# An S4D convolution and a feed-forward layer on one core: the kernel products take turns over the column tiles, in fewer steps

## The chip, the cores and the metric

The kernel runs on one NeuronCore of a Trainium2 chip. The metric is the device time of one execution in microseconds. The core has a matrix engine (PE, TensorE), which multiplies into PSUM, a vector engine (DVE), a scalar engine (ACT), GpSimd (POOL) and a queue engine (SP). In this kernel SP and POOL start nearly all transfers. Each engine takes its instructions in the order of the built program and waits on semaphores for the others.

## The reference

The input is 2048 tokens of 576 channels, all float32. Two residual stages follow each other, each modulated by rows of `silu(c) @ w_mod`:

```python
h = _layernorm(x) * (1 + ca) + sa
x = x + ga * _A_ref(h, ...)        # S4D: a convolution along the tokens, per channel
h = _layernorm(x) * (1 + cb) + sb
x = x + gb * _B_ref(h, w1, w2)     # relu(h @ w1) @ w2, with 4608 hidden units
```

The convolution kernel of a channel is `K[l] = 2 Re sum_n C[n] exp(A[n] dt l)` over 128 states n and 2048 positions l.

## The kernel before

**The convolution kernel K.** A position is split as l = 32 a + b. For one channel, K is a matrix product over the 128 states: `W2` (128 states x 32 values of b) times `W1` (128 states x values of a), once for the real parts and once for the imaginary parts (r = 0 and 1), added up in PSUM. The 576 channels are cut into 12 half groups h of 48 channels. A half group's 48 channels stand as 4 x 12: dd = 0 to 3 picks one of four column tiles of the matrix array (32 columns, 32 PSUM partitions each) and q = 0 to 11 is the place along the row. So a half group is 96 matmuls of 128 x 32 weights. The moving side has 16 columns for each block of 512 positions: 16, 32 or 48.

**Where these products run.** Block 0 of K (16 columns) is made first, by `products` of `KGen` (lines 252 to 269), before the feed-forward layer starts. Blocks 1 to 3 are made by `rest` (lines 383 to 475) beside the feed-forward layer: in feed-forward block 0 the half groups 0 to 5 with 48 columns (blocks 1, 2, 3) in turn with the half groups 6 to 11 with 16 columns (block 1); in feed-forward block 1 the half groups 6 to 11 with 32 columns (blocks 2, 3). Before its products a half group's `W1r` is rotated on DVE (`rot`, lines 403 to 415: two products of 1536 elements, an addition and a subtraction of 768). Its `W2r`, `W` and `Zr` are loaded by POOL's queue. ScalarE copies the products out of PSUM into `ker` (line 450), and when six half groups are done POOL's queue stores them.

**The convolution.** `conv` (line 855) transforms, multiplies spectra (`product`, line 970), and transforms back, for token blocks of 512; block s + 1 is convolved beside feed-forward block s.

**The feed-forward layer.** `ffn` (line 1246) goes through 4 token blocks of 36 hidden tiles. One tile is 14 matmuls into `hps` (line 1305) and 14 into five accumulators `acc` (line 1330), each 128 x 512, with operands split into a high and a low part (`xh`, `xl`, `hh`, `hl`). ScalarE writes `hh` (line 1310), DVE `hl` (line 1311); the second buffer of `hps` comes free with `hl`.

**What sets the order.** The side work is a generator per block. `step` (line 1340) is called every seven feed-forward matmuls and takes pieces from the generator until the work done reaches a rate (2.3 units per step in block 0, 1.85 in block 1). A piece that yields a number counts that many units (its DVE time). A piece that yields `None` is a piece of matrix work: it counts 0.7, and a step takes at most two of them. Behind that a scheduler of the language orders the instructions of each engine. The PSUM tag `cps` has one buffer in this stage, so a new tile of `kps` waits for the ScalarE copy of the one before.

Of the kernel before, what the change touches and what calls it, by code (L numbers as in the profile page):

```python
# [10 lines left out]
F32 = mybir.dt.float32  # L11
F32R = mybir.dt.float32r
I32 = mybir.dt.int32
AF = mybir.ActivationFunctionType
# [4 lines left out]
P = 128  # L19
# [21 lines left out]
def strips(t, k):  # L41

    w = t.shape[1] // k
    return bass.AP(tensor=t.tensor, offset=t.offset, ap=[[w, P], [P * w, k], [1, w]])


class KGen:
# [204 lines left out]
    def products(self, ps, W1, W2, u, between):  # L252

        for q in range(12):
            if q % 6 == 3:
                for _ in range(2):
                    next(between, None)
            for dd in range(4):
                ch = dd * 12 + q
                for r in range(2):  # L260
                    self.mm = self.kept(
                        self.nc.tensor.matmul(  # L262
                            ps[32 * dd : 32 * dd + 32, 12 * u + q, :],
                            W2[:, r, :, ch],
                            W1[:, u, :, r, ch],
                            start=(r == 0),
                            stop=(r == 1),
                        )
                    )
# [113 lines left out]
    def rest(self, psum, items, beside=iter(())):  # L383


        nc, k = self.nc, self.k
        v = nc.vector.tensor_tensor
        kes, rows = {}, {}
        most = 16 * max(len(blocks) for _, blocks in items)
        with ExitStack() as ctx:  # L390
            pt = k.pool(ctx, f"kr{items[0][1][0]}")

            def load(h):
                W2 = pt.tile([P, 2, 32, H], F32, tag="W2", bufs=2, name=f"W2r_{h}")
                W0 = pt.tile([P, 16, 2, H], F32, tag="W0", bufs=2 if most == 48 else 1, name=f"W0_{h}")
                Z = pt.tile([P, 2, 2, H], F32, tag="Z", bufs=2, name=f"Zr_{h}")
                d = nc.gpsimd.dma_start
                d(out=W0.rearrange("p (y a) r c -> p y (a r c)", y=2), in_=strips(k.W1d[h], 2))
                d(out=Z.rearrange("p i r c -> p (i r c)"), in_=k.Zd[h])
                k.gate = d(out=W2.rearrange("p r (y b) c -> p (r y) (b c)", y=2), in_=strips(k.W2d[h], 4))  # L400
                return W2, W0, Z

            def rot(out, X, Z, i):
                cb = [P, 32, H]
                flat = "p a r c -> p (a r) c"
                T = pt.tile([P, 16, 2, H], F32, tag="T", name="T")
                zr, zi = (Z[:, i, r].unsqueeze(1).broadcast_to(cb) for r in range(2))
                v(T.rearrange(flat), X.rearrange(flat), zi, op=ALU.mult)
                yield 1.75
                v(out.rearrange(flat), X.rearrange(flat), zr, op=ALU.mult)  # L410
                yield 1.75
                v(out[:, :, 0], out[:, :, 0], T[:, :, 1], op=ALU.subtract)  # L412
                yield 0.95
                v(out[:, :, 1], out[:, :, 1], T[:, :, 0], op=ALU.add)
                yield 0.95

            def rots(W1, W0, Z, blocks):
                a = [W1[:, 16 * i : 16 * i + 16] for i in range(len(blocks))]
                if blocks[0] == 1:
                    yield from rot(a[0], W0, Z, 0)  # L420
                    if len(blocks) > 1:
                        yield from rot(a[1], W0, Z, 1)
                        yield from rot(a[2], a[0], Z, 1)
                else:
                    yield from rot(a[0], W0, Z, 1)
                    yield from rot(a[1], a[0], Z, 0)

            def products(h, W1, W2, blocks):
                na = 16 * len(blocks)
                key = (h // 6, blocks)  # L430
                if key not in kes:
                    kes[key] = pt.tile([P, na, 72], F32, name=f"ker_{h}")
                ke = kes[key]
                for half in range(2):
                    ps = psum.tile([P, 6, na], F32, tag="cps", bufs=1, name="kps")
                    for q in range(6):
                        for dd in range(4):
                            ch = dd * 12 + 6 * half + q
                            for r in range(2):
                                nc.tensor.matmul(  # L440
                                    ps[32 * dd : 32 * dd + 32, q, :],
                                    W2[:, r, :, ch],
                                    W1[:, :na, r, ch],
                                    start=(r == 0),
                                    stop=(r == 1),
                                )
                        if q == 2:
                            yield None
                    q0 = 12 * (h % 6) + 6 * half
                    nc.scalar.activation(  # L450
                        ke[:, :, q0 : q0 + 6], ps.rearrange("p q a -> p a q"), AF.Copy
                    )
                    yield None
                rows[key] = rows.get(key, 0) + 1
                if rows[key] == 6:
                    yield -1
                    for i, s in enumerate(blocks):
                        self.store(
                            s, h // 6, ke[:, 16 * i : 16 * i + 16].rearrange("p a q -> p (a q)"),
                            nc.gpsimd,  # L460
                        )

            nxt = load(items[0][0])
            yield -1
            prev = iter(())
            for i, (h, blocks) in enumerate(items):
                W2, W0, Z = nxt
                W1 = pt.tile([P, most, 2, H], F32, tag="W1", bufs=2, name=f"W1r_{h}")
                yield from spread(rots(W1, W0, Z, blocks), prev, len(blocks))
                if i + 1 < len(items):  # L470
                    nxt = load(items[i + 1][0])
                prev = products(h, W1, W2, blocks)
                if i + 2 == len(items):
                    yield next(beside, -1)
            yield from both(prev, beside)


def spread(a, b, n):

    for i, w in enumerate(a):  # L480
        yield w
        if i % n == n - 1:
            yield next(b, 0.0)
    yield from b


class Body:
# [20 lines left out]
    def v(self, *args, **kw):  # L508
        return self.kept(self.nc.vector.tensor_tensor(*args, **kw))  # L509
# [982 lines left out]
def both(a, b):  # L1492

    while True:
        n = 0
        for g in (a, b):
            for w in g:
                n = 1
                yield w
                break  # L1500
        if not n:
            return
# [58 lines left out]
```

## Time and profile before

| | us |
|---|---|
| runs: lowest, median, highest (3 runs) | 1362.56, 1365.63, 1367.47 |
| profiled execution: from the first to the last instruction (span) | 1360.4 |
| what the median run has beyond that span | 5.2 |
| matmuls busy (PE), weight loads busy (PEld) | 1226.0, 973.7 |
| vector engine, scalar engine, GpSimd busy | 871.4, 503.5, 195.3 |
| products of line 440: matmul records, busy | 3456, 77.4 |
| products of line 262: matmul records, busy | 2304, 40.3 |

The profiled execution's own time is known as its span, from its first to its last instruction. The runs were timed by themselves and hold what lies around it.

A matmul of two float32 operands stands in the trace as two matmul records, each with a weight load of its own; one of the feed-forward layer (`fp32r`) as one. So the 1728 matmuls of line 440 are 3456 records. A row of the timeline joins equal instructions that follow each other: its start, its length to the end of the last one, and how many. In brackets stands how long the engine idled before it and who ended the wait; "issue" means that the engine waited for nothing that the profile shows. The ends of matmuls are modelled, so the starts are the surer times. Rows of the stage view give a stretch, its length, then the busy time and the instructions of each engine, the granted clock, the share of the transfer engines and GB/s.

### The profile page before, as it was taken

Reading aid. Unit: us, or ns where it says so; the run is one execution under the profiler, and the core shown is the slowest. Engines: PE = TensorE matmul, PEld = TensorE weight load, DVE = VectorE, ACT = ScalarE, POOL = GpSimd, SP = SyncE. Lnnn points to the kernel's source line nnn. Section 1 sums busy time; section 2 is a strip of 40 time slices with the busy share of each in tenths; the row PEclk is TensorE's granted clock in tenths of the full one; section 3 lists DMA queues with packets and bytes.
Section 4 is the critical chain, followed back from the end, with each engine's and each line's share of the span. In section 5 each row is a group of like instructions: output and inputs, shape, how many; then the busy total and the mean of one; then the engine's idle time right before and its main releaser. Section 6 shows DMA issues by size and latency. Waiting matters only on the chain.

```text
span 1360.4 us, 26053 instructions
## 1 busy us (share of the span) xinstructions
PE 1226.0 (90%) x10608; PEld 973.7 (72%) x10608; DVE 871.4 (64%) x1351; ACT 503.5 (37%) x1014; POOL 195.3 (14%) x271
## 2 busy tenths in 40 slices
PE   5125797999999987999999999999999999999998
PEld 3124565777787766777777887787888888888886
DVE  5978997998878698469737986266999222111111
ACT  7986234222224311622233225333322253233321
POOL 1777231111120100021101100100010000000000
PEclk9557899999999998999999999999999999999999
DMA  6666499988898755699689894677997567666651
GB/s 196 243 246 241 135 356 366 331 292 275 292 344 289 265 199 207 205 362 316 236 278 342 294 362 143 206 245 233 317 348 259 178 177 211 198 195 197 197 174 61
DMA packets 132424, 340.47 MB, mean 250 GB/s; under 512 B 22352, under 2 KB 22672, under 8 KB 132304
## 3 DMA queue, kind: packets, MB, share of 16 engines
q1 hardware_dynamic: 105200, 215.21, 48.9%
q0 software_dynamic: 26816, 123.01, 24.6%
q8 instruction: 83, 1.36, 0.4%
q10 hardware_dynamic: 288, 0.59, 0.1%
q14 instruction: 37, 0.30, 0.1%
HBM read 258.55 MB, written 80.22 MB: 249 GB/s over the span
## 4 chain that ended last, share of the span: by engine, by line
PE 70%; DVE 11%; DMA 10%; issue 4%; ACT 2%; POOL 1%; SPq 0%; DVEq 0%; ACTq 0%; POOLq 0%
PE acc L1330 28%; PE hps L1305 28%; PE kps L440 5%; PE ps_f L757 4%; PE kps L262 3%; DVE T L509 2%; DVE Y L509 2%; DMA Ua<-Ud 2%; DMA Ud<-U 2%; DVE k L133 1%; PE ps_i L998 1%; DMA h<-in_x_dram 1%; DMA Ka<-Rd 1%; DMA Zr<-Zd 1%; DMA W1d<-W 1%
## 5 line engine op out<-in xcount | busy, mean ns | idle before, releaser
L1330 PE MATMUL acc<-hh,w 128*128 128x512 f32 x1296 | 422.1, 400 | 0.3 <-DVE w L509 0.3
L1305 PE MATMUL hps<-xh,w 128*128 128x512 f32 x1152 | 394.3, 402 | 4.4 <-ACT xh L1061 3.5
L1311 DVE SCALAR_TENSOR_TENSOR hl<-hps,hh 128x512 fp32r<-128x512 f32 x144 | 99.0, 688 | 291.3 <-ACT hh L1310 291.0
L1330 PEld LDWEIGHTS acc<-hh,w 128*128 128x128 f32 x1296 | 242.1, 188 | 52.5 <-DVE w L509 0.9
L1330 PE MATMUL acc<-hl,w 128*128 128x512 f32 x720 | 278.7, 399 | 0.0
L1305 PEld LDWEIGHTS hps<-xh,w 128*128 128x128 f32 x1152 | 217.4, 190 | 52.1 <-ACT xh L1061 4.7
L1305 PE MATMUL hps<-xl,w 128*128 128x512 f32 x576 | 230.8, 401 | 0.2 <-DVE xl L1066 0.2
L1310 ACT ACTIVATE hh<-hps 128x512 fp32r<-128x512 f32 x144 | 86.0, 598 | 354.6 <-PE hps L1305 347.0
L1283 ACT ACTIVATE w<-r 128x576 fp32r<-128x576 f32 x144 | 98.6, 686 | 217.9 <-issue 168.4
L1330 PEld LDWEIGHTS acc<-hl,w 128*128 128x128 f32 x720 | 135.3, 188 | 28.2
L1305 PEld LDWEIGHTS hps<-xl,w 128*128 128x128 f32 x576 | 109.2, 190 | 24.8 <-DVE xl L1066 1.5
L1305 PE MATMUL hps<-xs,w 128*128 128x512 f32 x288 | 97.2, 417 | 14.3 <-DVE hl L1311 14.0
L1276 ACT ACTIVATE w<-r 128x640 fp32r<-128x640 f32 x142 | 104.0, 733 | 12.4 <-DMA r<-in_w_dram 12.4
L262 PE MATMUL kps<-W,W 128*32 128x16 f32 x2304 | 40.3, 215 | 71.5 <-POOL W L59 47.3
L262 PEld LDWEIGHTS kps<-W,W 128*32 128x32 f32 x2304 | 37.9, 150 | 76.2 <-POOL W L59 49.7
L440 PEld LDWEIGHTS kps<-W1r,W2r 128*32 128x32 f32 x3456 | 68.4, 146 | 30.7 <-issue 16.8
L509 DVE TENSOR_TENSOR Y<-Y,T 128x1152 f32<-128x1152 f32 x64 | 84.7, 1351 | 0.2
L440 PE MATMUL kps<-W1r,W2r 128*32 128x48 f32 (+2 forms) x3456 | 77.4, 238 | 7.0 <-DVE W1r L412 3.3
L1305 PEld LDWEIGHTS hps<-xs,w 128*128 128x128 f32 x288 | 52.8, 190 | 28.3 <-DVE hl L1311 17.1
L758 ACT ACTIVATE Z<-ps_f 128x288 f32<-128x288 f32 x104 | 42.4, 407 | 63.1 <-PE ps_f L757 62.3
L509 DVE TENSOR_TENSOR w<-r,w 128x512 fp32r<-128x512 f32 (+2 forms) x108 | 57.9, 572 | 8.6 <-ACT w L1283 8.6
L509 DVE TENSOR_TENSOR W<-Z 128x576 f32<-128x576 f32 x52 | 37.1, 752 | 29.3 <-ACT Z L758 29.3
(216 smaller groups left out, 1362.8 us busy)
## 6 DMA issues: line engine op xcount, KB each, us to landing
r<-in_w_dram SPq DMA_DIRECT2D x144, 320.0 KB, 4.2
r<-in_w_dram SPq DMA_DIRECT2D x144, 288.0 KB, 3.7
w<-L1d SPq DMA_DIRECT2D x108, 320.0 KB, 3.0
w<-L2d SPq DMA_DIRECT2D x108, 288.0 KB, 3.2
W2r<-W2d POOLq DMA_DIRECT2D x18, 1536.0 KB, 9.4
W2d<-W SPq DMA_DIRECT2D x10, 1536.0 KB, 7.4
W<-W1d POOLq DMA_DIRECT2D x18, 768.0 KB, 8.9
Ua<-Ud POOLq DMA_DIRECT2D x12, 1152.0 KB, 10.3
```

Of the source, the lines that this page charges most:

```text
L133: self.nc.vector.scalar_tensor_tensor(f[:, i].rearrange(pair, u=2), th, float(slot), k[:, i].rearrange(pair, u=2), op0=ALU.mult, op1=ALU.s ...
L262: self.nc.tensor.matmul(ps[32 * dd : 32 * dd + 32, 12 * u + q, :], W2[:, r, :, ch], W1[:, u, :, r, ch], start=(r == 0), stop=(r == 1),)
L440: nc.tensor.matmul(ps[32 * dd : 32 * dd + 32, q, :], W2[:, r, :, ch], W1[:, :na, r, ch], start=(r == 0), stop=(r == 1),)
L509: return self.kept(self.nc.vector.tensor_tensor(*args, **kw))
L757: kept(nc.tensor.matmul(o, fc[:, n2, c, :], src(n2), start=True, stop=True))
L758: nc.scalar.activation(Z[:, n2, c], ps[:, :PC], AF.Copy)
L1276: nc.scalar.activation(w[:, 0], r, AF.Copy)
L1283: nc.scalar.activation(w[:, 0:D], r2[g], AF.Copy)
L1305: nc.tensor.matmul(ps, a, x, start=(i == 0), stop=(i == 13))
L1310: nc.scalar.activation(hh, ps, AF.Relu)
L1311: nc.vector.scalar_tensor_tensor(hl, ps, 0.0, hh, op0=ALU.max, op1=ALU.subtract)
L1330: nc.tensor.matmul(acc[i], a, x, start=(f == 0 and j in (0, 3, 6, 9, 12)), stop=(f == NF - 1 and j in (2, 5, 8, 11, 13)),)
```

## The change

In both places the loops over r and dd change places: each matmul now goes to another column tile than the one before, and the r = 1 matmul of a channel comes four matmuls after its r = 0. In `rest`, a half group with 16 or 32 columns now has one PSUM tile of 12 x 16 or 12 x 32 and one step (96 matmuls, one copy); one with 48 columns has two tiles of 6 x 48 and two steps (48 matmuls each). Before, every half group had two tiles, two copies and four steps of 24 matmuls.

```diff
@@ products @@
-            for dd in range(4):
-                ch = dd * 12 + q
-                for r in range(2):
+            for r in range(2):
+                for dd in range(4):
+                    ch = dd * 12 + q
                     self.mm = self.kept(
@@ rest @@
-                for half in range(2):
-                    ps = psum.tile([P, 6, na], F32, tag="cps", bufs=1, name="kps")
-                    for q in range(6):
-                        for dd in range(4):
-                            ch = dd * 12 + 6 * half + q
-                            for r in range(2):
+                n = 12 if na < 48 else 6
+                for q1 in range(0, 12, n):
+                    ps = psum.tile([P, n, na], F32, tag="cps", bufs=1, name="kps")
+                    for q in range(n):
+                        for r in range(2):
+                            for dd in range(4):
+                                ch = dd * 12 + q1 + q
                                 nc.tensor.matmul(
                                     ps[32 * dd : 32 * dd + 32, q, :],
                                     W2[:, r, :, ch],
...
-                        if q == 2:
-                            yield None
-                    q0 = 12 * (h % 6) + 6 * half
+                    q0 = 12 * (h % 6) + q1
                     nc.scalar.activation(
-                        ke[:, :, q0 : q0 + 6], ps.rearrange("p q a -> p a q"), AF.Copy
+                        ke[:, :, q0 : q0 + n], ps.rearrange("p q a -> p a q"), AF.Copy
                     )
                     yield None
```

The lines behind it move up by one (1305 becomes 1304, 1330 becomes 1329, 1311 becomes 1310), the matmul of `rest` is at line 441 after the change.

How this moves the instructions is seen in the built order. First TensorE at the first half group with 16 columns, beside the second hidden tiles of feed-forward block 0 (the last column is partitions x columns and the number of matmuls). Before:

```order
L440 MATMUL kps<-W1r_2947,W2r_2927 32x48 x48
L1305 MATMUL hps<-xh_2777,w_2987 128x512
L1305 MATMUL hps<-xl_2778,w_2987 128x512
L1305 MATMUL hps<-xh_2777,w_2987 128x512
L440 MATMUL kps<-W1r_3032,W2r_3026 32x16
L1330 MATMUL acc_0_3035<-hl,w_2997 128x512
...
L1330 MATMUL acc_0_3035<-hh,w_3138 128x512 x2
L440 MATMUL kps<-W1r_3032,W2r_3026 32x16 x47
L1305 MATMUL hps<-xs_2779,w_3024 128x512 x2
L440 MATMUL kps<-W1r_3032,W2r_3026 32x16 x24
```

and after the change, at the same place:

```order
L441 MATMUL kps<-W1r_2947,W2r_2927 32x48 x48
L1304 MATMUL hps<-xh_2777,w_2987 128x512 x2
L1304 MATMUL hps<-xl_2778,w_2987 128x512
L441 MATMUL kps<-W1r_3032,W2r_3026 32x16 x4
L1304 MATMUL hps<-xh_2777,w_2987 128x512
L441 MATMUL kps<-W1r_3032,W2r_3026 32x16 x92
L1329 MATMUL acc_0_3035<-hl,w_2997 128x512
```

The half group's 96 matmuls stood in four pieces (1, 47, 24 and 24) between feed-forward matmuls, and now stand in two, of 4 and 92, close behind the 48-column half group. Over the whole program the runs of line 440 go from 65 to 39.

Second DVE, at the second spectral product (`Y_1`) of token block 1, between two writes of `hl`, for which the feed-forward matmuls wait. Before:

```order
L1311 SCALAR_TENSOR_TENSOR hl<-hps,hh 128x512
L509 TENSOR_TENSOR w_6016<-r_5889,w_6016 128x64
L509 TENSOR_TENSOR w_6016<-r_5889,w_6016 128x512
L509 TENSOR_TENSOR x_1_5270<-ps_i,x_1_5270 128x4x72
L509 TENSOR_TENSOR Y_1_5951<-K_1_1_5909,Ua 128x4x288 x2
L509 TENSOR_TENSOR T<-K_1_1_5909,Ua 128x1152 x2
L509 TENSOR_TENSOR Y_1_5951<-Y_1_5951,T 128x4x288 x2
L509 TENSOR_TENSOR T<-R,U_1_5469 128x1152
L509 TENSOR_TENSOR w_5987<-r_5954,w_5987 128x640
L509 TENSOR_TENSOR Y_1_5951<-Y_1_5951,T 128x4x288
L509 TENSOR_TENSOR T<-R,U_1_5469 128x1152
L1311 SCALAR_TENSOR_TENSOR hl<-hps,hh 128x512
```

and after the change, from the first instruction behind the earlier `hl`:

```order
L508 TENSOR_TENSOR Y_1_5833<-K_1_1_5778,Ua 128x4x288 x2
L508 TENSOR_TENSOR T<-K_1_1_5778,Ua 128x1152 x2
L508 TENSOR_TENSOR Y_1_5833<-Y_1_5833,T 128x4x288 x2
L508 TENSOR_TENSOR T<-R,U_1_5346 128x1152 x2
L508 TENSOR_TENSOR Y_1_5833<-Y_1_5833,T 128x4x288 x2
L508 TENSOR_TENSOR T<-R,U_1_5346 128x1152
L508 TENSOR_TENSOR w_5918<-r_5794,w_5918 128x64
L508 TENSOR_TENSOR w_5918<-r_5794,w_5918 128x512
L508 TENSOR_TENSOR w_5889<-r_5855,w_5889 128x640
L508 TENSOR_TENSOR Y_1_5833<-Y_1_5833,T 128x4x288
L508 TENSOR_TENSOR T<-R,U_1_5346 128x1152
L1310 SCALAR_TENSOR_TENSOR hl<-hps,hh 128x512
```

Three more of the large instructions of 1152 elements now stand between the two writes of `hl`, because the side work of this block is taken up earlier: the last product of line 440 in feed-forward block 0 stands at its feed-forward matmul 473 instead of 526 (of 1008).

## The prediction

> **What bounds the kernel now.** I read the page first, then the stages, then the rows of the products themselves. The page's busy times, queues and chain:
>
> ```profile
> PE 1226.0 (90%) x10608; PEld 973.7 (72%) x10608; DVE 871.4 (64%) x1351; ACT 503.5 (37%) x1014; POOL 195.3 (14%) x271
> q8 instruction: 83, 1.36, 0.4%
> PE 70%; DVE 11%; DMA 10%; issue 4%; ACT 2%; POOL 1%; SPq 0%; DVEq 0%; ACTq 0%; POOLq 0%
> ```
>
> Then three stretches of the stage view (us, then busy time and instructions of PE, PEld, DVE, ACT and POOL, then clock, DMA share, GB/s):
>
> ```profile
> 242.00:271.00 29.00, 27.79 (x461) 22.13 (x462) 29.00 (x31) 7.88 (x15) 4.28 (x7) 1.00 0.89 321
> 230.00:404.00 174.00, 168.93 (x2760) 133.84 (x2761) 157.79 (x175) 40.85 (x75) 25.22 (x39) 1.00 0.88 311
> 404.00:1360.00 956.00, 929.97 (x5137) 743.31 (x5131) 526.07 (x746) 322.29 (x574) 61.32 (x85) 0.99 0.73 239
> ```
>
> From 230 us on TensorE sets the end: it idles 5 us of the first 174 and 26 of the other 956. A microsecond taken from its queue there is a microsecond of the kernel, and one added likewise, unless DVE is the tighter one: between 242 and 271 us it has no gap at all. Before 230 us the chain runs elsewhere, and the products of that part (line 262) are no bound by their arithmetic:
>
> ```profile
> 112.92 2.36 PE L262 MATMUL kps<-W,W 128*32 128x16 f32 x128 [1.56 <-issue]
> 116.49 2.11 PE L262 MATMUL kps<-W,W 128*32 128x16 f32 x128 [1.21 <-issue]
> 120.22 2.13 PE L262 MATMUL kps<-W,W 128*32 128x16 f32 x127 [1.62 <-issue]
> 123.93 1.26 PE L262 MATMUL kps<-W,W 128*32 128x16 f32 x72 [1.58 <-issue]
> ```
>
> Each fp32 matmul of the program is two records on PE and two on PEld. 128 records run in 2.1 us, then PE stands still for 1.2 to 1.6 us with no releaser, and starts again 3.6 to 3.7 us after the last start. The instruction queue explains it: 83 fetches for 10608 + 10608 instructions are 256 each, that is 128 matmul records with their weight loads. **A long run of short matmuls outruns the instruction fetch**, one batch per 3.7 us.
>
> The same in the feed-forward stage, where the runs of line 440 stand between matmuls of lines 1305 and 1330:
>
> ```profile
> 252.93 1.64 PE L440 MATMUL kps<-W1r,W2r 128*32 128x16 f32 x94
> 254.50 0.73 PE L1305 MATMUL hps<-xs,w 128*128 128x512 f32 x2
> 255.16 0.94 PE L440 MATMUL kps<-W1r,W2r 128*32 128x16 f32 x48
> 256.03 0.50 PE L1305 MATMUL hps<-xh,w 128*128 128x512 f32 x1
> 256.36 0.39 PE L1305 MATMUL hps<-xl,w 128*128 128x512 f32 x1
> 256.59 0.63 PE L1305 MATMUL hps<-xh,w 128*128 128x512 f32 x2
> 257.06 0.39 PE L1305 MATMUL hps<-xl,w 128*128 128x512 f32 x1
> 257.38 0.59 PE L440 MATMUL kps<-W1r,W2r 128*32 128x16 f32 x19
> 259.15 0.68 PE L440 MATMUL kps<-W1r,W2r 128*32 128x16 f32 x29 [1.18 <-issue]
> 283.42 0.73 PE L1305 MATMUL hps<-xh,w 128*128 128x512 f32 x2 [0.89 <-issue]
> 347.31 0.59 PE L440 MATMUL kps<-W1r,W2r 128*32 128x16 f32 x19 [1.36 <-issue]
> ```
>
> Counted in the program's order, 768 PE instructions lie between the stops at 259.15 and 283.42 and 2048 between the latter and 347.31: 3 and 8 batches of 256. So these stops are batch edges too. They cost 3.4 us (1.18 + 0.89 + 1.36) in all.
>
> **The change part by part.**
>
> *Taking turns.* In the old order four records follow each other on one column tile. On one tile two records start 0.08 (16 columns) to 0.10 us (48 columns) apart, which two short rows and the mean durations give (0.29 - 0.21, 0.36 - 0.27):
>
> ```profile
> 279.75 0.29 PE L440 MATMUL kps<-W1r,W2r 128*32 128x16 f32 x2
> 243.16 0.36 PE L440 MATMUL kps<-W1r,W2r 128*32 128x48 f32 x2
> L440 PE MATMUL kps<-W1r,W2r 128*32 128x48 f32 x1152 | 30.7, 266 | 0.0
> L440 PE MATMUL kps<-W1r,W2r 128*32 128x16 f32 x1152 | 23.8, 212 | 2.5 <-issue 2.5
> 276.36 2.33 PE L440 MATMUL kps<-W1r,W2r 128*32 128x48 f32 x96
> ```
>
> If tiles waited for each other in program order, three of four steps would cost that, 60 to 75 ns on average. The x94 row at 252.93 gives (1.64 - 0.21) / 93 = 15 ns and the x96 row (2.33 - 0.27) / 95 = 22 ns. The four tiles already run side by side, each through its own list, and the change leaves each tile's own list as it was. I cost the rotation at nothing in both places; in line 262 the fetch hides it besides. Beside the rows stands a rule of the Trainium skill (TensorE: Matmul & The Clock Gate, Part 3, The mechanism): matmuls start and end strictly in program order. By it the old order would lose three tiles of four and the rotation would win them back, worth far more than all else here; the 15 ns disagree with it.
>
> *Fewer runs.* The order has 65 runs of line 440 between feed-forward matmuls before, and 39 after. What a run costs beside its pairs comes from one of 48 records and one of 96, of 32 columns, between single feed-forward rows:
>
> ```profile
> 633.93 0.39 PE L1330 MATMUL acc<-hl,w 128*128 128x512 f32 x1
> 634.25 0.97 PE L440 MATMUL kps<-W1r,W2r 128*32 128x32 f32 x48
> 635.15 0.73 PE L1305 MATMUL hps<-xs,w 128*128 128x512 f32 x2
> 635.72 0.39 PE L1305 MATMUL hps<-xh,w 128*128 128x512 f32 x1
> 642.52 0.39 PE L1330 MATMUL acc<-hl,w 128*128 128x512 f32 x1
> 642.84 1.68 PE L440 MATMUL kps<-W1r,W2r 128*32 128x32 f32 x96
> 644.45 0.73 PE L1305 MATMUL hps<-xs,w 128*128 128x512 f32 x2
> ```
>
> 635.15 - 633.93 = 1.22 us and 644.45 - 642.52 = 1.93 us: 48 more records cost 0.71 us (15 ns each). A feed-forward step takes 0.23 us, and the two after the run 0.57 instead of 0.46. So a run of 48 costs 1.22 - 0.23 + 0.11 = 1.10 us, of which 0.39 is not its pairs. 26 runs fewer: **-10 us** (without the 0.11: -7).
>
> *Longer runs meet the fetch.* A 16- or 32-column half group is now 368 or 384 instructions in a row (92 or 96 matmuls, one row of the order) and in block 0 follows the 48-column one after four feed-forward matmuls. Counted back 256 instructions, the batch that ended at 259.15 began near 253.5: 5.6 us for one batch. I put the batch edges where the stops above put them (both programs have the same instruction count up to the products), walk both orders with 0.23 us, 15 and 22 ns and the 0.39, and let an edge come no sooner than a fixed time after the one before. With 3.7 us (the head's rows) the old order waits 2 us in all and the new one 12; with 4.5, 8 and 21. The old one's measured 3.4 asks for about 4.0, which gives the new one 15. So **+12 us**, from +8 to +13, and down to +4 if the fetch starts earlier than I assume.
>
> *Pace.* Each step counts 0.7 in the planner's budget; 30 steps fewer (48 to 18 in block 0) are 21 units, at 2.3 a step nine steps, so block 0's side work ends some 65 feed-forward matmuls sooner. No wait stood at that block's end, so this gains nothing. It packs DVE: with the durations of the rows, DVE work between two hl writes rises from 9.0 to about 9.9 us while the products run (PE there: about 10.2 with the fetch). The other place that can pay is the second spectral product of token block 1, which runs beside feed-forward block 0:
>
> ```profile
> 508.80 0.46 DVE L509 TENSOR_TENSOR x<-ps_i,x 128x288 f32<-128x288 f32 x1
> 512.05 2.63 DVE L509 TENSOR_TENSOR Y<-K,Ua 128x1152 f32<-128x1152 f32 x2 [2.79 <-DMA Ua<-Ud]
> 524.95 1.22 PE L1305 MATMUL hps<-xs,w 128*128 128x512 f32 x2 [4.81 <-DVE hl L1311]
> PE hps L1305 <- DVE hl L1311: 14.0, 7, 4.8
> ```
>
> Behind the hl on DVE, TensorE's next hps waits. The new order puts 17.9 instead of 13.4 us of DVE work between these two hl writes, but less in the next gap (8.1 for 10.4): **+2 us**, from 0 to +5.
>
> *Clock.* Stops can cost more than themselves:
>
> ```profile
> 525.00:530.00 5.00, 5.00 (x15) 4.04 (x16) 5.00 (x5) 0.00 (x0) 0.00 (x0) 0.66 0.00 0
> 535.00:540.00 5.00, 3.96 (x9) 3.02 (x10) 5.00 (x11) 0.00 (x0) 0.00 (x0) 0.52 0.56 218
> 536.04 1.22 PE L1305 MATMUL hps<-xs,w 128*128 128x512 f32 x2 [2.81 <-DVE hl L1311]
> ```
>
> After stops of 4.81 and 2.81 us the granted clock is 0.66 and 0.52 over 5 us, 1.7 to 2.4 us lost; after 1.18 us it stayed 1.00 (first stretch). The walk's waits are mostly 1.5 to 2.5 us, so one such fall: **+1.5 us**, from 0 to +8. The Trainium skill (same page, the table under Why this matters for your kernels) draws the line at idle gaps over about 3 us; by it none of the new stops would cost clock and the sum is 1.5 less. The fall after 2.81 us lies just below that line.
>
> *Evacuation.* 12 copies of the products on ScalarE fall away (36 to 24). ScalarE is busy 41 of 174 us, so nothing.
>
> Sum: -10 + 12 + 2 + 1.5 = +5.5. The profiled span of 1360.4 becomes 1365.9. The median of the runs lies 5.2 over that span (1365.6), so **1371 us**.
>
> **The rivals.** *The fetch keeps up* (B): a trigger early enough would hide the longer runs, as it hides most of today's edges. For it: only three edges show today. Against: the head, where every edge shows. Time: -10 + 2 = -8, 1358. *Rotation speeds the pairs* (C): each of 2304 narrow and 1152 wide records at 10 ns for 15 and 22 would save 25 us, of which the fetch lets through perhaps half: 1350 with the fewer runs. Against it speaks the side-by-side running; the rule above is what speaks for it. *DVE decides* (D), the slower mechanism: from the point where DVE work per hl exceeds PE's time in the same gap, TensorE waits for hl. At the place shown that is 4.5 us on top of 4.81, two more such gaps in block 0 and their clock falls: about +15 in all, 1381. DVE without a gap at 242 to 271 speaks for it, the 157.8 of 174 us against. *The change does little* (E): where DVE is the tighter one the shorter queue on TensorE only waits, and half of the saving goes there, the rest to the fetch: 1365.
>
> **How the numbers follow.** 0.3% is 4.1 us, about what a measurement here can tell from no change. My forecast (A) 0.52, with its own range from 1363 to 1378: slower 0.37, same 0.14, faster 0.01. B 0.22: faster 0.19, same 0.03. C 0.06 faster. D 0.10 slower. E 0.10 same. Together faster 0.26, same 0.27, slower 0.47. The range takes in B and D: 1356 to 1381.
>
> **What would show it.** Right: rows of line 441 of about 184 records, or cut in two by a stop "<-issue" of 1.5 to 3 us; "issue" before kps and before the next feed-forward matmul growing from 3.4 to 10 us and more; records still 15 and 22 ns apart; line 262 still 3.7 us per 128 records; the last product of block 0 before feed-forward matmul 480 instead of 530. Wrong: pairs closer than 15 ns (C), no stop inside the long rows (B), or "PE hps <- DVE hl" beyond 20 us (D).

## The result and the profile after

| kernel | median of the runs, us (lowest to highest) | ratio to the kernel before, 95% interval |
|---|---|---|
| before (timed beside it) | 1365.63 (1362.56 to 1370.72, 5 runs) | 1 |
| changed | 1383.68 (1382.12 to 1387.53, 5 runs) | 1.0138 [1.0119, 1.0157] |

The change makes the kernel slower by 18 us, three times the 5.5 us forecast and beyond the upper end of the range (1381). The profiled span is 1381.9 instead of 1360.4 us; the execution profiled of before was a quick one, so that the traces differ by 21.5 us where the medians differ by 18. The page's busy times, instruction queue and chain of the changed kernel:

```profile
PE 1223.9 (89%) x10608; PEld 976.9 (71%) x10608; DVE 870.8 (63%) x1351; ACT 502.4 (36%) x1002; POOL 194.3 (14%) x271
q8 instruction: 83, 1.36, 0.4%
PE 68%; DVE 15%; DMA 8%; issue 6%; ACT 2%; POOL 1%; SPq 0%; DVEq 0%; ACTq 0%; POOLq 0%
```

TensorE has 2 us less work, the instruction queue the same 83 fetches, and the share of "issue" in the chain went from 4 to 6%. The stage view of the changed kernel for the three stretches of the prediction (columns as there):

```profile
242.00:271.00 29.00, 22.57 (x434) 18.08 (x435) 29.00 (x31) 5.82 (x11) 4.57 (x7) 0.88 0.82 283
230.00:404.00 174.00, 153.67 (x2542) 122.59 (x2542) 153.67 (x167) 34.71 (x61) 24.01 (x37) 0.94 0.79 289
404.00:1360.00 956.00, 927.02 (x5262) 743.57 (x5261) 525.18 (x747) 323.98 (x571) 62.54 (x88) 0.99 0.73 242
```

In the first 174 us of the feed-forward stage TensorE now idles 20 us instead of 5, and its clock is 0.94 instead of 1.00. The page's group row of the products, of before and of the changed kernel:

```profile
L440 PE MATMUL kps<-W1r,W2r 128*32 128x48 f32 (+2 forms) x3456 | 77.4, 238 | 7.0 <-DVE W1r L412 3.3
```

```profile
L441 PE MATMUL kps<-W1r,W2r 128*32 128x48 f32 (+2 forms) x3456 | 69.4, 238 | 31.9 <-issue 26.2
```

The second is the changed kernel's. The products themselves became 8 us cheaper, and the idle time before them grew by 25. The waits of TensorE in the changed kernel (total, times, longest):

```profile
PE kps L441 <- issue: 26.2, 10, 6.1
PE hps L1304 <- DVE hl L1310: 7.8, 7, 1.8
PE acc L1329 <- DVE w L508: 4.2, 1, 4.2
```

Stops without a releaser were 3.4 us and are 26.2: eight of the ten, 25.9 us, stand in 16- or 32-column rows, the other two are of 0.18 us each at 48-column rows. The wait for hl fell from 14.0 to 7.8. One of the long rows on TensorE's timeline:

```profile
247.64 2.32 PE L441 MATMUL kps<-W1r,W2r 128*32 128x48 f32 x96
...
251.45 2.70 PE L441 MATMUL kps<-W1r,W2r 128*32 128x16 f32 x169
260.25 0.43 PE L441 MATMUL kps<-W1r,W2r 128*32 128x16 f32 x15 [6.10 <-issue]
260.62 2.50 PE L1329 MATMUL acc<-hl,w 128*128 128x512 f32 x5
```

169 records take 2.70 us, (2.70 - 0.21) / 168 = 14.8 ns each, and the 96 wide ones (2.32 - 0.27) / 95 = 21.6 ns: the pace of before (15 and 22). Then TensorE stands still for 6.10 us, and behind the stop five feed-forward matmuls take 2.50 us, half the usual speed.

That these stops belong to the instruction fetch can be counted. With the records of TensorE's sequencer counted too, TensorE resumes at all eight at an instruction 193 or 194 beyond a multiple of 256, as at the three stops of before, and 2.2 to 2.6 us after a packet of the instruction queue has started (the two stops of 0.18 us fit neither). Such a place, where a fetched batch of 256 instructions begins, is called an edge below.

In the head nothing changed:

```profile
109.99 2.12 PE L262 MATMUL kps<-W,W 128*32 128x16 f32 x127 [1.51 <-issue]
113.82 2.11 PE L262 MATMUL kps<-W,W 128*32 128x16 f32 x128 [1.71 <-issue]
117.44 2.09 PE L262 MATMUL kps<-W,W 128*32 128x16 f32 x128 [1.52 <-issue]
```

Since the 4032 feed-forward matmuls come in the same order in both, the time from the 62nd to the last can be split by what stood at each place (sums over the trace, us; "slow" is what feed-forward matmuls more than 0.27 us apart take beyond 0.23):

```
            total   stops over 0.3   rows of products   feed-forward (slow)   other
before     1117.1        23.6             72.8             958.0 (42.0)        62.7
changed    1138.4        47.2             66.6             962.5 (48.3)        62.1
```

Of the 21 us, 23.6 are stops (whoever ended them), 4.5 slower feed-forward matmuls, and 6.2 came back in the rows of products.

### The profile page after: what moved, and what is told of

It is laid out like the page before. It is cut to its first block, busy times and chain, and to the rows that moved or that the text cites. A ratio compares the mean times of both kernels' runs of the same rounds, so it can differ in the third digit from the quotient of the medians.

```text
span 1381.9 us, 26040 instructions
## 1 busy us (share of the span) xinstructions
PE 1223.9 (89%) x10608; PEld 976.9 (71%) x10608; DVE 870.8 (63%) x1351; ACT 502.4 (36%) x1002; POOL 194.3 (14%) x271
## 4 chain that ended last, share of the span: by engine, by line
PE 68%; DVE 15%; DMA 8%; issue 6%; ACT 2%; POOL 1%; SPq 0%; DVEq 0%; ACTq 0%; POOLq 0%
PE hps L1304 27%; PE acc L1329 26%; PE kps L441 4%; PE ps_f L756 4%; DVE T L508 3%; PE kps L262 3%; DVE Y L508 3%; DMA Ua<-Ud 2%; DMA Ud<-U 1%; DVE k L133 1%; PE ps_i L997 1%; DVE T L408 1%; DMA Zr<-Zd 1%; DVE W1r L410 1%; DMA kt<-kd 1%
## 5 line engine op out<-in xcount | busy, mean ns | idle before, releaser
L1329 PEld LDWEIGHTS acc<-hh,w 128*128 128x128 f32 x1296 | 245.4, 191 | 57.3 <-DVE w L508 4.9
L441 PE MATMUL kps<-W1r,W2r 128*32 128x48 f32 (+2 forms) x3456 | 69.4, 238 | 31.9 <-issue 26.2
L441 PEld LDWEIGHTS kps<-W1r,W2r 128*32 128x32 f32 x3456 | 62.9, 147 | 46.9 <-issue 34.6
L1304 PEld LDWEIGHTS hps<-xs,w 128*128 128x128 f32 x288 | 53.9, 192 | 23.4 <-DVE hl L1310 11.1
## 6 DMA issues: line engine op xcount, KB each, us to landing
W2r<-W2d POOLq DMA_DIRECT2D x18, 1536.0 KB, 10.6
```

What stands on the lines that cost most here:

```text
L441: nc.tensor.matmul(ps[32 * dd : 32 * dd + 32, q, :], W2[:, r, :, ch], W1[:, :na, r, ch], start=(r == 0), stop=(r == 1),)
L1304: nc.tensor.matmul(ps, a, x, start=(i == 0), stop=(i == 13))
L1329: nc.tensor.matmul(acc[i], a, x, start=(f == 0 and j in (0, 3, 6, 9, 12)), stop=(f == NF - 1 and j in (2, 5, 8, 11, 13)),)
```

## The experiments

All times in one table: ratios against the kernel before timed in the same series; "stops" is the time for which TensorE idled before products or feed-forward matmuls with no releaser, and the longest, both from one profile. Most of these stops are edges by the count above. Nine of the profiles also have one of 0.5 to 2.3 us at the start of a 32-column half group, in another place of the count, whose cause the traces don't show.

| kernel | median, us | ratio, 95% interval | stops, longest |
|---|---|---|---|
| before | | 1 | 3.4, 1.4 |
| changed | 1383.68 | 1.0138 [1.0119, 1.0157] | 26.2, 6.1 |
| turns alone | 1361.74 | 0.9970 [0.9951, 0.9989] | 5.1, 2.0 |
| steps alone | 1382.72 | 1.0119 [1.0091, 1.0147] | 29.0, 4.9 |
| halves | 1383.80 | 1.0130 [1.0101, 1.0158] | 19.5, 4.9 |
| one tile, 24 a step | 1362.82 | 0.9979 [0.9959, 0.9999] | 6.4, 2.8 |
| long rows, old count | 1378.34 | 1.0096 [1.0063, 1.0129] | 25.9, 4.3 |
| halves, old count | 1373.80 | 1.0070 [1.0042, 1.0098] | 14.1, 3.2 |
| 24 a step, new count | 1376.41 | 1.0106 [1.0068, 1.0144] | 12.6, 4.1 |
| turns, side work early | 1363.91 | 1.0009 [0.9990, 1.0028] | 14.8, 3.3 |
| changed, no W2r loads | 1371.30 | 1.0048 [1.0019, 1.0077] | 17.2, 3.5 |
| before, no W2r loads | 1358.85 | 0.9963 [0.9940, 0.9987] | 1.4, 0.5 |
| long rows, old count, no W2r loads | 1360.03 | 0.9977 [0.9955, 0.9998] | 12.4, 2.2 |
| wide 48, narrow 24 a step | 1361.86 | 0.9991 [0.9972, 1.0010] | 6.1, 3.2 |
| the same, one step a call | 1406.07 | 1.0298 [1.0262, 1.0333] | 12.0, 3.0 |
| turns, one step a call | 1406.45 | 1.0295 [1.0264, 1.0325] | 11.1, 3.6 |

The theory after the result, which the runs below test: the long rows outrun the instruction fetch by more than forecast, and the rest is small. Below, a per cent of the ratio is taken as 13.64 us.

**1. The two parts apart.** The turns alone: in the kernel before, only

```diff
-for dd in range(4):
-    for r in range(2):
+for r in range(2):
+    for dd in range(4):
```

> The kernel before with the r and dd loops changed over in both places; four steps per half group and two tiles as before. Theory (the long rows outrun the instruction fetch, and the turns themselves cost nothing): 1362 to 1367 us, within 0.3% of before, stops of TensorE before kps of 2 to 6 us in all and none above 2 us, records 14.7 and 21.6 ns apart. Rival 1 (the turns themselves cost time, for instance because the r = 1 matmul now comes four matmuls behind its r = 0): 1375 us or more, with the long stops. Rival 2 (the turns gain what the change then loses elsewhere): 1355 or less.

The steps alone: the changed kernel with these two loops put back.

> The changed kernel with the old order of the loops (dd outside, r inside) in both places, but one or two steps per half group as in the change. Theory: 1380 to 1390 us like the change, stops before kps of 20 to 28 us in all, inside the 16- and 32-column rows. Rival 1 (the turns cost): 1368 or less. If the turns shorten the stops or lengthen them by more than 5 us in all, the order on the column tiles matters to the fetch.

The groups of the products by shape with the turns alone, and its waits:

```profile
L440 PE MATMUL kps<-W1r,W2r 128*32 128x48 f32 x1152 | 29.5, 266 | 0.7 <-issue 0.7
L440 PE MATMUL kps<-W1r,W2r 128*32 128x16 f32 x1152 | 22.3, 211 | 3.9 <-issue 3.9
L440 PE MATMUL kps<-W1r,W2r 128*32 128x32 f32 x1152 | 22.2, 237 | 4.6 <-DVE W1r L412 4.1 <-issue 0.6
```

The waits with the steps alone:

```profile
PE kps L441 <- issue: 29.0, 11, 4.9
```

The loss is the steps' whole: +16 us without the turns. The turns alone make a kernel that is faster than both, by 4 us (1.5 to 6.7), and the rows show it: the three groups take 74.0 us where they took 77.4. I had put that at nothing. Together with the steps the gain doesn't show (1.0138 with the turns, 1.0119 without; the intervals overlap).

**2. Shorter rows.** Halves: every half group in two steps of 48 matmuls.

```diff
-n = 12 if na < 48 else 6
+n = 6
```

> The changed kernel with two tiles and two steps of 48 matmuls for every half group, also those of 16 and 32 columns (n = 6 always): 36 steps where before had 72 and the change 24. Theory: a row is at most 96 records, 192 instructions, and feed-forward matmuls stand between, so the fetch has time to land: stops before kps of 4 to 10 us in all, 54 runs instead of 65 save 4 us, so 1360 to 1370 us. Rival 3 (it is the coarser counting of steps that packs DVE's work and costs the time, not the fetch): three quarters of the change's loss, 1376 to 1382, with the stops small.

One tile and one copy as in the change, but a step after every 24 matmuls:

```diff
+                        if q % 3 == 2 and q + 1 < n:
+                            yield None
                     q0 = 12 * (h % 6) + q1
```

> The changed kernel with one tile and one copy per half group of 16 or 32 columns, but a step after every 24 matmuls as before (72 steps). Theory: the tile and the copy cost nothing, so 1360 to 1368 us, stops before kps under 7 us in all. Rival 4 (the one large tile holds up the next products until its copy is done, since the tag has one buffer): 1375 or more, with waits before kps for ker.

The waits with halves:

```profile
PE kps L441 <- issue: 19.0, 11, 4.9
PE hps L1304 <- DVE hl L1310: 14.1, 9, 4.9
```

The waits with the single tile and steps of 24:

```profile
PE kps L441 <- issue: 6.1, 3, 2.8
PE hps L1306 <- DVE hl L1312: 14.0, 7, 4.8
```

The single tile is as good as the turns alone, so tile and copy cost nothing. The halves miss: the loss of the whole change with 7 us less of stops. The stops of 19.5 us are twice what I expected (two halves mostly stand one to three feed-forward matmuls apart), but they are not all of it, and the number of steps, which the planner counts, had to be tried by itself.

**3. The planner's count.** The rows of the change, but a step counts what the steps that it replaces counted, by a number of its own kind that the planner adds to its work done:

```diff
-                    yield None
+                    yield complex(0, 0.7 * (n // 3))
@@ step @@
+                elif isinstance(w, complex):
+                    pe += 1
+                    done[0] += w.imag
```

> The changed kernel with its long rows, but a step of n x 4 matmuls counts in the planner's budget what the steps it replaces counted (0.7 for every 12 of n's 3 x 4, so 2.8 for 96 matmuls and 1.4 for 48), so that the side work stands where it stood before. Theory (the fetch stops cost the time; the earlier side work by itself wins some 13 us back at the waits for hl between feed-forward matmul 850 and 1130, which the change shows and this kernel then lacks): stops before kps of 20 to 28 us, 1383 to 1397 us. Rival 3 (the coarser counting packs DVE and costs the time): 1362 to 1370.

The same with halves (1.4 for each):

> The changed kernel with two steps of 48 matmuls for every half group (as in the run of halves), each counting 1.4 in the planner's budget, so that the side work stands where it stood before. Two halves still stand only one to three feed-forward matmuls apart. Theory (rows and their neighbours set the fetch stops; the earlier side work adds some 5 us more): stops before kps of 12 to 20 us and 1368 to 1377 us. Rival 3 (the halves' loss of 1.3% is the earlier side work alone): 1366 or less.

The other way round, steps of 24 matmuls which together count 0.7 a tile (`yield complex(0, 2.1 / n)` after each):

> The changed kernel with a step after every 24 matmuls (rows as short as before, one tile and one copy as in the change), but the steps of a tile count together 0.7 as in the change, so that the side work stands as early as in the change. Theory: stops before kps of 4 to 10 us like before, and the gain at the waits for hl between feed-forward matmul 850 and 1130 stays: 1348 to 1360 us. Rival 3 (the earlier, denser side work costs the time): 1374 us or more with few stops.

And the turns alone, old steps and tiles, with the side work of block 0 put as early as in the change:

```diff
             target = self.rate(g // NF) * (at[0] % 144 or 144)
+            if g < NF:
+                target += min(21.0, 0.28 * at[0])
```

> The turns alone with the short rows of before, and the planner's target in feed-forward block 0 raised step by step by up to 21 units, the count that the change's fewer steps leave out, so that the side work stands as early as in the change while the rows keep their 24 to 48 matmuls. Theory (earlier side work costs by itself, by waits of TensorE for DVE and ACT and by more products per stretch): 4 to 9 us above the turns alone, 1365 to 1371 us, stops before kps below 9 us. Rival 8 (early side work costs only where the rows are long, and otherwise wins at the waits for hl between feed-forward matmul 850 and 1130): 1362 us or less.

How much later than in the kernel before a feed-forward matmul starts in the profiled executions (us):

```
feed-forward matmul         500    850   1130   1400   last
changed                    28.4   26.3   13.2   22.1   21.5
long rows, old count        9.0    9.6    8.2   18.2   16.8
24 a step, new count       21.3   19.8    9.6    8.2   13.1
turns, side work early     23.0    9.5    1.2    0.3   -0.9
turns alone                 1.4    2.2    1.2    0.6    0.5
```

The early side work loses 20 us in block 0 (some 8 of it are products that only come sooner). By matmul 1130 the turns with early side work have won nearly all of it back, the changed kernel about half. What it costs in the end, four pairs of runs say: 5.7 us with the long rows (1.0138 against 1.0096), 8.2 with halves (1.0130 against 1.0070), 5.3 with short rows (1.0009 against 0.9970; early in block 0 only), and 17.3 with one tile and 24 a step (1.0106 against 0.9979). The pairs come from different series, and the first one's intervals overlap a little. That early side work costs time, all four show; how much depends on the rest of the order. In the fourth pair the wait for hl stays at 14.4 us, where the turns with early side work have 4.4, and the loss of block 0 isn't won back by matmul 850; why, stays open, and for that kernel rival 3 is not refuted. The run with short rows and the one with halves at the old count fall within or near what the theory gave them (1373.8 for 1368 to 1377; 1363.9 for 1365 to 1371, with more stops than the 9 us expected). The long rows at the old count lie between theory (1383 to 1397) and rival 3 (1362 to 1370): I had expected them to lose the gain at hl; the wait there is indeed longer, yet the kernel is faster. The waits with the long rows and the old count:

```profile
PE kps L441 <- issue: 25.9, 9, 4.3
PE hps L1304 <- DVE hl L1310: 11.6, 5, 8.8
```

And with the turns and early side work:

```profile
PE kps L440 <- issue: 10.0, 6, 3.3
PE acc L1330 <- issue: 2.4, 1, 2.4
PE hps L1305 <- issue: 2.4, 1, 2.4
```

Early side work sets the products closer together, and with short rows that alone brings the stops from 5.1 to 14.8 us; likewise in the steps of 24 with the new count (12.6), where the planner put two and more of them into one row: they were to come to 1348 to 1360 us and take 1376, as rival 3 had it, though not with few stops. With the old count the long rows still cost 13 us against before and 17 against the turns alone: the fetch (eight edges with 23.9 of the 25.9 us of stops, where the turns alone have three with 4.6).

**4. Why a stop lasts so long.** The W2r loads of all but the first two half groups of each list are left out:

```diff
+                new = len(W2s) < 2
-                W2 = pt.tile(...)
+                W2 = pt.tile(...) if new else W2s[-2]
+                W2s.append(W2)
...
-                k.gate = d(out=W2.rearrange(...), in_=...)
+                k.gate = d(out=Z.rearrange(...), in_=...)
+                if new:
+                    k.gate = d(out=W2.rearrange(...), in_=...)
```

In the changed kernel:

> The changed kernel with W2r loaded only for the first two half groups of each list (14 loads of 1.5 MB are left out and the later half groups multiply by the wrong weights, so the products are wrong; every instruction of TensorE stays). Theory (a stop is long because the fetch of the next batch waits behind those loads): stops before kps fall from 26 us to 8 to 14 and none is above 3 us, about 1360 to 1368 us. Rival 5 (a stop's length is the fetch's own cycle, whatever else is transferred): stops stay above 20 us with single ones above 4, 1378 us or more.

In the kernel before:

> The kernel before with the same 14 loads of W2r left out (wrong products, the same instructions of TensorE): what the missing loads do by themselves. Theory: the stops were 3.4 us and fall to about 1, so 1360 to 1366 us, and the kernel without loads and with long rows comes within 6 us of it. Rival 5: 1360 to 1366 too, but the one with long rows stays 15 us or more above it.

With the long rows and the old count:

> Long rows as in the change, the planner's count as before (as in the run of the pace), and the 14 loads of W2r left out (wrong products, the same instructions of TensorE). With the run of the pace and the two runs without loads it fills a square of rows by loads at one pace. Theory (a stop has two parts, the fetch's own cycle of about 3.7 us and a wait behind the loads): stops before kps of 12 to 18 us, none above 3.6, 1363 to 1370 us: 5 to 10 us above the kernel before without loads, and 8 to 15 below the same rows with loads. Rival 9 (at the old pace the loads alone make the stops): within 3 us of the kernel before without loads.

The waits of the three, in this order:

```profile
PE kps L446 <- issue: 17.2, 7, 3.5
```

```profile
PE kps L445 <- issue: 1.0, 2, 0.5
```

```profile
PE kps L446 <- issue: 12.4, 10, 2.2
```

The first lies between the theory (8 to 14 us of stops, 1360 to 1368) and rival 5 (above 20, 1378): 17.2 us and 1371, 12.5 us above the second, of which the early side work is a part. The third shows it at the old count. One of its rows on TensorE's timeline:

```profile
251.53 2.62 PE L446 MATMUL kps<-W1r,W2r 128*32 128x16 f32 x163
256.32 0.54 PE L446 MATMUL kps<-W1r,W2r 128*32 128x16 f32 x21 [2.18 <-issue]
256.79 0.74 PE L1309 MATMUL hps<-xs,w 128*128 128x512 f32 x2
257.37 0.40 PE L1309 MATMUL hps<-xh,w 128*128 128x512 f32 x1
```

The same row with its loads (the run of long rows and old count):

```profile
251.36 2.62 PE L441 MATMUL kps<-W1r,W2r 128*32 128x16 f32 x163
257.69 0.54 PE L441 MATMUL kps<-W1r,W2r 128*32 128x16 f32 x21 [3.71 <-issue]
258.16 1.22 PE L1304 MATMUL hps<-xs,w 128*128 128x512 f32 x2
259.18 0.63 PE L1304 MATMUL hps<-xh,w 128*128 128x512 f32 x1
```

Same row, same edge: 2.18 us and full speed behind it, or 3.71 us and half speed. In the changed kernel the fetch's own packets show where the time goes (us; the times of the packets are read from the trace):

```
TensorE stops   fetch packet starts   TensorE resumes
   254.15            257.69               260.25
   313.49            315.71               318.23
   372.91            374.23               376.47
   407.73            408.12               410.47
   630.26            631.04               633.58
   678.62            678.93               681.47
```

From the packet's start to the next matmul it is always 2.2 to 2.6 us. What varies is when the packet starts. Two fetches are never nearer than 3.2 us, mostly 3.5 to 3.7 where they follow at once. Among the products the shortest delays are mostly 0.4 to 0.9 us, counted from the moment at which TensorE has passed some 170 instructions beyond a multiple of 256. I put the request there. That is an estimate which the trace doesn't show, and beside feed-forward matmuls alone some packets start up to 2 us before that moment. From the same point the 257.69 fetch took 5.8 us. This is POOL's row of the changed kernel just before:

```profile
250.27 0.77 POOL L400 DMA_DIRECT2D W2r<-W2d  x1 [1.92 <-PE kps L441]
```

The 1.5 MB load is set off by the end of the products before, so it runs beside the next row. A W2r load was still under way when the packet started at the three longest stops (6.10, 4.74 and 3.56 us, 14.4 in all); at the other five edges, 11.5 us, it had landed, and other transfers ran. The mean from that point to the packet, over the fetches beside products, is about 2.6 us before, 3.7 in the changed kernel, 1.6 before without the loads, 2.6 to 2.9 (by which fetches are taken in) with long rows and old count without them.

At the old count, the square of rows and loads reads, in us against before: short rows with loads 0 (-4 with the turns), long with loads +13; short without loads -5, long without -3. So long rows, with the turns in them, cost 13 us with the loads (9 to 18 by the intervals) and 2 without (-2 to 6, not clear of nothing). My 5 to 10 was too much, rival 9 has the time right. But it isn't right that the loads alone make the stops: 12.4 us of them remain, in ten stops of at most 2.2 us. Nine of these, 10.4 us, are edges; the tenth, 2.06 us, resumes 9.3 us after the last fetch packet. Against the short rows without loads (and without the turns) the profile has 10.6 us more of stops between the 62nd and the last feed-forward matmul; the rows of products give 5.5 back, the feed-forward matmuls 8.0, 2.2 of it at half clock.

The Trainium skill (Runtime: NRT & Kernel Launch, Instruction fetch mechanics) says that the sequencer fetches blocks of 256 instructions ahead through a queue of its own, and that crossing a block is mostly hidden. The blocks agree (83 fetches); mostly hidden holds for the rows of before and not here, where the eight edges in long rows cost 0.5 to 6.1 us each.

**5. Toward a better order.** Wide half groups in steps of 48, narrow ones in steps of 24, old count:

> The turns in both places; 48-column half groups in two steps of 48 matmuls (counting 1.4 each, as what they replace), 16- and 32-column ones in four steps of 24 (0.7 each) with one tile and one copy. Two steps per call of the planner as before, and the side work where it stood before. Theory (only long rows of short records outrun the fetch, the wide rows have 22 ns per record and leave it time): stops before kps of 3 to 7 us, all in narrow rows, 1357 to 1364 us, not above the turns alone by more than 2 us. Rival 7 (rows of 48 matmuls stop whatever their width): new stops in the 48-column rows and 1366 or more.

The same with `pe < 1` for `pe < 2` in the planner's loop, so one step of matrix work a call; and that with the turns alone:

> The changed kernel with one step of 48 matmuls per tile for the 48-column half groups (counting 1.4), four steps of 24 for the narrow ones (0.7 each, one tile, one copy), and at most one step of products in each call of the planner instead of two, so that feed-forward matmuls stand between nearly all rows. Theory: the batches land in time, stops before kps of 0 to 4 us, 1353 to 1361 us. Rival 6 (spreading the products puts the side work of feed-forward block 1 late, its last products some 40 feed-forward matmuls later, and costs more than the stops): 1366 or more.

> The kernel before with the turns, its four steps and two tiles, and at most one step of products in each call of the planner instead of two. Theory: stops before kps of 0 to 3 us, 1354 to 1361 us, below the turns alone by 1 to 5 us. Rival 6 (late side work costs): 1366 or more.

The first is no better than the turns alone: 0.9991, stops 6.1 us. The second and third fail by 41 us:

```profile
PE ps_i L999 <- DVE V L510: 29.3, 4, 15.5
PE kps L441 <- issue: 12.0, 6, 3.0
```

```profile
PE ps_i L998 <- DVE V L509: 32.4, 3, 18.6
PE kps L440 <- issue: 11.1, 6, 3.6
```

The limit also holds for the matrix pieces of the convolution, which then ends late: TensorE waits up to 15.5 and 18.6 us for the inverse transform's V. Rival 6 has the time and that side work comes late, but it named the late products of block 1 and not the convolution. The stops were to fall to 4 us or less and are 12 and 11: spreading rows of 48 evenly doesn't hide the fetch. Why these edges show and those with the turns alone mostly don't, I haven't settled.

## Why the prediction was wrong

The place of the loss and the mechanism were right: rows of 184 are cut by stops at the edges, line 262 keeps its 3.6 to 4.8 us per batch, "issue" grew beyond 10. (The last product of block 0 does come before feed-forward matmul 473, but the built order had already shown that.) By its steps:

- **Longer runs meet the fetch, +12 (to +13): measured +22.8 (26.2 - 3.4).** This is the step that failed. The walk let "an edge come no sooner than a fixed time after the one before", with 4.0 us fitted to three stops of before. That holds the fetch's own cycle (3.5 to 3.7) and hardly a wait. At the three longest stops, with a W2r load under way, TensorE went on 5.8 to 8.4 us after the point where I put the request, and the loads are issued when the products before them end, beside the next row. The prediction had the sign of it in hand, the batch that took 5.6 us at 259.15, and set it aside for a mean of 4.0; by the same count all three stops of before took 5.8 to 6.0.
- **Clock, +1.5 (to +8): about +9.5.** Feed-forward matmuls that start at half clock take 5.1 us beyond 0.23 each in the kernel before, 9.6 with the turns alone (two stops of 1.96 and 1.91 us) and 14.6 in the changed kernel. The 42.0 to 48.3 of the split has in it slow places at full clock, which became fewer. The waits were not "mostly 1.5 to 2.5"; of the changed kernel's eight stretches of half clock between 230 and 700 us six came with the stops at edges. The stage view, 5 us behind the stops of 6.10 and 4.74 in the changed kernel:

```profile
260.00:265.00 5.00, 4.75 (x25) 3.79 (x26) 5.00 (x7) 1.01 (x2) 1.45 (x2) 0.50 0.77 225
318.00:323.00 5.00, 4.77 (x39) 3.87 (x40) 5.00 (x6) 1.01 (x2) 1.45 (x2) 0.50 1.04 359
```

- **Fewer runs, -10 (to -7): about -8.** From the turns alone to the changed kernel the rows of products, taken as in the split, fall by 2.8 us and the feed-forward matmuls outside half clock by 5.0.
- **Taking turns, 0: measured -4** (section 1). That the tiles run side by side was right; the old order still lost about 1 ns a record (3.4 us over 3456).
- **Pace, 0 and +2 at the second spectral product: +5 to +8 in three pairs of runs, +17 in the fourth, and not at that place.** There the wait for hl fell (14.0 to 7.8) and 13 us came back; the cost is in block 0, where more products meet the fetch and TensorE waits for DVE and ACT.
- **Evacuation, 0:** right (the single tile).

The split accounts for the 21.3 us between the two traces: +23.6 stops, +9.5 half clock, -5.0 feed-forward matmuls at full clock, -6.2 rows of products, -0.6 other. The pace isn't a further term there, since its cost shows as stops and half clock. The forecast had +14 of stops (fetch and pace) and +1.5 of clock. So the longer stops are the largest miss, the fall of the clock behind them the second, and the turns came out better than forecast. All this is read from one profile of each kernel. The 5.2 us that the forecast put between span and median were no fixed part: the changed kernel's profiled execution took 1383.7 us, 1.8 beyond its span of 1381.9, and the rest of the 5.2 came from the quick execution that was profiled of before.

Rival D named nearly the right time (1381) by the wrong way: the hl wait shrank. Rival B fell with the first stop. Rival C had the sign of the turns, but 3.4 us in the rows for its 25.

## What to carry to other kernels

A long row of short matmuls has to be priced with the instruction fetch as it is in that stage, under its transfers; the stops of another stage don't give the price (1.2 to 1.6 us a batch in rows of the head, up to 6.1 beside the feed-forward layer). Before rows are made longer, look which loads their end sets off: here the same rows cost 13 us beside 1.5 MB loads, and without them 2, which is not clear of the noise. And a step that a planner counts is also a clock: merge steps and everything else moves, so give the merged step the sum of what it replaces, and try each half of a change alone, since here one half was a gain.

## What the runs showed of the hardware that was not expected

- Fetches of 256 instructions that follow at once start mostly 3.5 to 3.7 us apart, in no profile less than 3.2. At the edges of all sixteen profiles 2.2 to 2.7 us lie between the packet's start and the next matmul. At the three longest stops of the changed kernel, beside W2r loads, the packet started 3.6 to 5.8 us after the point where I put its request.
- Four column tiles run side by side in either order, yet turning from tile to tile took the rows from 77.4 to 74.0 us.
- How long a stop must be for the clock to fall isn't one number, since the clock is set on a grid. The stage view with the turns alone, behind a stop of 1.96 us that ended at 258.61, and with long rows without loads, from just before the end of the stop of 2.18 us:

```profile
259.00:264.00 5.00, 5.00 (x30) 4.01 (x24) 5.00 (x6) 1.48 (x3) 1.46 (x2) 0.66 1.03 347
```

```profile
256.00:261.00 5.00, 4.68 (x39) 3.92 (x40) 5.00 (x5) 1.00 (x3) 0.70 (x1) 1.00 0.76 248
```

0.66 after the shorter, 1.00 after the longer. The line of about 3 us in the Trainium skill (TensorE: Matmul & The Clock Gate, Why this matters for your kernels) doesn't divide these two. The traces' record of the granted clock does: in all sixteen profiles the clock changes only at multiples of 3.413 us from one another. With the turns alone the stop (256.65 to 258.61) lies whole in the stretch from 256.43 to 259.84, and the clock is halved from 259.84 on. With long rows without loads the edge of a stretch at 255.02 cuts the stop (254.15 to 256.32) into 0.87 and 1.30 us, and the clock stays. From 230 us on, no stretch at full clock in which TensorE idled less than 1.1 us in all was followed by half clock, and every one with more than 1.95 us was; in between both occur, and what decides there was not found.
